# Output product of the state rows: from one full product per row half to seven half-size products

## The chip, the cores and the metric

The kernel runs on one core of a Trainium2 chip. A core has TensorE (PE: matrix products, with a separate weight load PEld that overlaps the products), VectorE (DVE), ScalarE (ACT), GpSimd (POOL) and SyncE (SP, which issues DMAs here); each engine works through its own instructions in program order and waits on semaphores for the others. The metric is the time of one execution on the device in microseconds; less is better.

## The reference

Two stages: a cross attention between 512 token rows and 32 state rows, for 8 batches and 8 heads of 64, and then a gated feed-forward layer over all 4352 rows (8 x 544) of width 512, with an inner width of 1536.

```python
a = softmax(x @ state.T / 8)          # 512 x 32 for each batch and head
xread = a @ state                     # 512 x 64
a2 = softmax(state @ x.T / 8)         # 32 x 512
sread = a2 @ x                        # 32 x 64: the state rows
rows = concatenate([xread, sread])    # 544 rows a batch, 512 wide over the heads
gate = 1 / (1 + exp(-(rows @ w_gate)))
out = (gate * (rows @ w_val)) @ w_out # 4352 x 512, float32
```

## The kernel before, in words

The program is written in a fixed order: what stands first in the code is issued first on its engine, and nothing reorders it. Batches 0 to 7 of token rows are followed by a ninth "batch" `b == B` (B is 8), which holds the state rows of all eight batches together: 8 x 32 = 256 rows. `step(b, f)` handles one of the 12 blocks of 128 of the inner width for one batch. For `b == B` it issues the two products of gate and value (`gv_half`, four matmuls of 256 columns each, line 388), the tanh on ScalarE (`gv_th`, line 394) and the gated product on VectorE (`gv_glu`, line 406, two instructions of 128 columns); the result is `glus[B]`, with 12 blocks of 256 rows.

Between these, every step carries a piece of the output product of the batch before it, so that for `b == B` it is the output product of batch 7. For batches 1 to 7 this is not done as one product: the rows (two halves of 256), the inner width (even and odd blocks f) and the output columns (two halves of 256) are each cut in two, and the eight products of quarters are replaced by seven (`prod`, `w_mm`; Winograd's form). That needs sums of quarters of the weights (`T`, made once by `t_sum`), sums of quarters of the glu blocks (`Sm`, four of them, `s_sum`, line 448), and additions of products as they leave PSUM (`w_keep` on ScalarE, `w_add` on VectorE, line 474). The last product of batch 7's second half is cut in three parts (`p_mm`, line 485, `p_add`, line 491).

The state rows, 256 of them, get no such treatment. After the last step, `out_mm(B, k)` runs for k from 0 to 5: for each half c of 128 rows, 12 matmuls of 512 columns accumulate one PSUM tile (line 422), ScalarE halves it into SBUF (line 426), and SP stores the 256 KB (line 432). Batch 0, which `out_mm` also serves, has another order of k. Behind that come the last three parts of batch 7 (`p_mm(4, part)`), whose additions on VectorE and stores from ACT, SP and ACT are the end of the program. Ahead of `out_mm(B, ...)` stand one addition of batch 7 (`w_add(5, "U2", ...)`, line 474) and the two stores that it allows (line 505).

PSUM places have names: `GV` (two buffers, used by gate and value in turn), `SWP` (four), `OU` and `AT` (one each). In a step for `b == B` the value product of step f takes the `GV` buffer that the gated product of step f-1 has read, so TensorE waits for VectorE there.

Of the kernel before, what the change touches and what calls it, by code (L numbers as in the profile page):

```python
# [8 lines left out]
FP = mybir.dt.float32  # L9
BF = mybir.dt.bfloat16  # L10
AF = mybir.ActivationFunctionType
ALU = mybir.AluOpType
# [4 lines left out]
def kernel(  # L17
# [29 lines left out]
    fp = ctx.enter_context(tc.tile_pool(name="fp", bufs=3))  # L47
# [293 lines left out]
    def sw_wide(b, v, other=AT):  # L341

        if b not in SWs:
            SWs[b] = fp.tile((128, 2, 2, dff), BF, name="SW", bufs=2)
        lo = 768 * v
        for k, places in enumerate(((OU, other), (SWP, SWP), (SWP, SWP))):
            pss = [p[0].tile((128, 512), FP, name="swp", tag=p[1]) for p in places]
            if k < 2:
                sw_mm(pss, b, k, lo, 512, 0)
            else:  # L350
                sw_pair(pss, b, lo + 512, 256)
            for e in range(2):
                if k < 2:
                    sw_left[b, v, k, e] = (SWs[b][:, e, k, lo:lo + 512], pss[e])
                else:
                    sw_left[b, v, k, e] = (SWs[b][:, e, :, lo + 512:lo + 768], pss[e].rearrange("p (w n) -> p w n", w=2))

    def sw_cp(b, lo, w, e, cp):
        cp(*sw_left.pop((b, lo, w, e)))  # L359
# [50 lines left out]
    def rows_of(b, c):  # L410
        return out[b * SC:b * SC + S].rearrange("(p c) n -> c p n", c=4)[c]

    def out_mm(b, k, place=None):
        c, f0 = k // 3, (k % 3) * 4
        if b == 0:

            c, f0 = k // 6 * 2 + k % 2, k % 6 // 2 * 4
        if f0 == 0:
            place = place or (SWP if b == B else OU)
            ops[b, c] = place[0].tile((128, 512), FP, name="outp", tag=place[1])  # L420
        for f in range(f0, f0 + 4):
            nc.tensor.matmul(ops[b, c], glus[b][:, f, c * 128:(c + 1) * 128], wo[:, f],  # L422
                             start=(f == 0), stop=(f == NF - 1))
        if f0 == 8:
            res = fp.tile((128, 512), FP, name="res", bufs=3, padded_shape=(128, 1024))
            nc.scalar.activation(res, ops[b, c], AF.Copy, scale=0.5)
            if b < B:
                n = 512
                for lo in range(0, 512, n):
                    nc.sync.dma_start(rows_of(b, c)[:, lo:lo + n], res[:, lo:lo + n])  # L430
            else:
                nc.sync.dma_start(out.rearrange("(b s) n -> s b n", s=SC)[S:, 4 * c:4 * c + 4], res)

    def A(b, h, r):

        return glus[b].rearrange("p (i r) t -> p r i t", r=2)[:, r, :, h * 256:h * 256 + 256]
# [6 lines left out]
    def s_sum(b, t, half=None):  # L443

        i = slice(0, 6) if half is None else slice(3 * half, 3 * half + 3)
        a, c, op = ((A(b, 1, 0)[:, i], A(b, 1, 1)[:, i], ALU.add), (Sm[:, 0, i], A(b, 0, 0)[:, i], ALU.subtract),
                    (A(b, 0, 0)[:, i], A(b, 1, 0)[:, i], ALU.subtract), (A(b, 0, 1)[:, i], Sm[:, 1, i], ALU.subtract))[t]
        nc.vector.tensor_tensor(Sm[:, t, i], a, c, op)  # L448
# [39 lines left out]
    def p_add(name, part, j):  # L488

        c, lo, n = parts[part]  # L490
        nc.vector.scalar_tensor_tensor(w_res(B - 1, 1)[:, c, j * 256 + lo:j * 256 + lo + n], wps["p", part], 0.5,
                                       held["w", name][:, c, lo:lo + n], ALU.mult, ALU.add)

    wres = {}

    def w_res(b, h):
        if (b, h) not in wres:
            wres[b, h] = fp.tile((128, 2, 512), FP, name="res", bufs=3)
        return wres[b, h]
# [7 lines left out]
    lo_, hi_ = slice(0, 256), slice(256, 512)  # L507
# [373 lines left out]
    def step(b, f):  # L881

        nb, o = (b + 1 if b + 1 < B else None), b - 1
        v, early = f // 6, b == 2
        if nb and f in (0, 6):
            if v:
                rd_mm(nb, AT)
            if early and not v:
                sw_wide(nb, v)
            else:  # L890
                sw_six(nb, v)
            sw_cp(nb, v, 0, 1, act)
# [36 lines left out]
        if f == 7:  # L929
            held["w", "U4"] = fp.tile((128, 2, 256), FP, name="U4", bufs=1)  # L930
            w_add(5, "U2", held["w", "U4"])
        if f == 8 and b < B:
            w_add(7, "U4", w_res(o, 1)[:, :, hi_])
        if f == 9 and b == B:
            for part in range(3):
                p_add("U4", part, 1)
        if f == 10 and b < B:
            w_add(5, "U2", w_res(o, 0)[:, :, hi_])
            w_store(o, 0, nc.sync)
        if f == 11 and b < B:  # L940
            w_add(7, "U2", w_res(o, 1)[:, :, lo_])
            w_store(o, 1, nc.sync)
        if nb:
            if f in (3, 5):
                n_sum(nb, f // 5)
            if f == 6:
                rd_fin(nb)

        if early:
            sums = {0: ((1, None), (2, 1)), 1: ((3, 0),), 2: ((3, 1),)}  # L950
        elif nb:
            sums = {0: ((0, 1), (1, 1)), 1: ((2, 0), (3, 0)), 2: ((2, 1), (3, 1))}
        else:
            sums = {0: ((0, 1),), 1: ((1, 1),), 2: ((2, 0),), 3: ((2, 1),), 5: ((3, 0),), 6: ((3, 1),)}
        for t, i in sums.get(f, ()):
            s_sum(o, t, i)
        if b < B and f in ((9, 11) if b < 6 else (7, 9)):
            s_sum(b, (f - 7) // 2 - (b < 6), 0)

        if nb:  # L960
            if f == 3 + early:
                at_Eb(nb)
            if f == 3 + early or f == 5:
                n_mul(nb, f // 5, pool)
            if f == 3 * early and nb + 2 < B:
                load_x(nb + 2, nc.sync)
            if f == 6:
                aT_dma(nb, 0)
                aT_dma(nb, 1)
                rd_dma(nb)  # L970
                if nb + 1 < B:
                    cast_x(nb + 1, pool, 0, 4)
                    cast_x(nb + 1, pool, 4, 4)
                    at_xT_dma(nb + 1)
                    cast_xs(nb + 1, 0, 4)
                    cast_xs(nb + 1, 4, 4)
            if f == 8 and early:
                for q in range(3):
                    rd_dma(q)
# [7 lines left out]
    w_add(5, "U2", w_res(o, 0)[:, :, hi_])  # L987
    w_store(o, 0, nc.sync)
    w_store(o, 1, nc.sync, cols=hi_)
    for k in range(6):  # L990
        out_mm(B, k, (SWP, OU)[k // 3])
    for part, eng in enumerate((nc.scalar, nc.sync, nc.scalar)):
        c, lo, n = parts[part]
        p_mm(4, part)
# [32 lines left out]
```

## Time and profile before

| what | value |
|---|---|
| median of 3 runs | 214.67 us (214.22 to 215.29) |
| the profiled execution's own time | 214.09 us |
| its span in the trace | 212.3 us |
| granted TensorE clock | 1.0 throughout |
| TensorE busy | 206.2 us, 97% |
| VectorE busy | 158.2 us, 75% |
| ScalarE busy | 129.0 us, 61% |

The span is what the trace covers; 1.8 us of the execution lie around it. Rows of the trace give a start in microseconds from the span's start, a duration, the engine, the line of the kernel, the output and its inputs, how many instructions are merged, and in brackets how long the engine stood idle before it and what ended that. Matmuls are pipelined: one of 256 columns is shown with 273 ns, but the next one starts much earlier.

### The profile page before, as it was taken

How to read it: one execution, taken by the hardware profiler on the slowest of the kernel's cores; microseconds unless marked ns; L12 is line 12 of the kernel's file. 1: busy time of each engine (PE TensorE's matmuls, PEld its weight loads, DVE VectorE, ACT ScalarE, POOL GpSimd, SP SyncE). 2: the span in 40 equal slices, each digit the busy share in tenths (PEclk: the TensorE clock that was granted, in tenths of full speed). 3: DMA queues.
4: the chain of work that ended last, by engine and by line, in shares of the span. 5: the costliest groups of instructions: out<-in, count | busy, mean ns of one | idle time of the engine just before them, and what ended most of it. 6: DMA issues, size and time to landing. Idle time of an engine off the chain costs nothing.

```text
span 212.3 us, 5235 instructions
## 1 busy us (share of the span) xinstructions
PE 206.2 (97%) x2053; PEld 126.3 (59%) x2057; DVE 158.2 (75%) x300; ACT 129.0 (61%) x243; POOL 72.8 (34%) x101
## 2 busy tenths in 40 slices
PE   8998999999999999999999999999999999999992
PEld 3553433544665656666656565656566666788842
DVE  6796897686975779777976798688968778777621
ACT  4897696586877467855786578647864543333211
POOL 7999170259155304650446033802410000000000
PEclk9999999999999999999999999999999999999999
DMA  6999999685498235945911640247010400220043
GB/s 176 206 197 201 275 224 169 93 299 91 92 271 224 60 70 181 242 64 138 313 51 37 98 198 15 43 88 212 14 40 30 177 2 0 99 102 0 3 175 121
DMA packets 40152, 27.01 MB, mean 127 GB/s; under 512 B 23616, under 2 KB 37184, under 8 KB 40128
## 3 DMA queue, kind: packets, MB, share of 16 engines
q1 hardware_dynamic: 29376, 18.69, 33.4%
q0 software_dynamic: 10320, 7.67, 21.8%
q10 hardware_dynamic: 432, 0.33, 0.6%
q8 instruction: 16, 0.26, 0.5%
q14 instruction: 8, 0.07, 0.1%
HBM read 18.35 MB, written 8.91 MB: 128 GB/s over the span
## 4 chain that ended last, share of the span: by engine, by line
PE 89%; DMA 5%; POOL 3%; issue 1%; ACT 1%; DVE 0%; POOLq 0%; ACTq 0%
PE gvp L385 35%; PE outp L466 29%; PE outp L422 7%; PE gvp L388 5%; DMA wgv<-in_moe_w_gate_dram 5%; PE swp L306 4%; PE gvp L373 3%; PE swp L322 2%; POOL wgv L107 2%; PE Sp L154 1%; PE outp L485 1%; POOL xf L103 1%; PE rdp L282 1%; PE rdp L285 0%; ACT SW L359 0%
## 5 line engine op out<-in xcount | busy, mean ns | idle before, releaser
L394 ACT ACTIVATE th<-gvp 128x512 f32<-128x512 f32 (+1 forms) x108 | 62.1, 577 | 52.5 <-PE gvp L385 36.2
L385 PE MATMUL gvp<-aT,SW 128*128 128x512 bf16 x352 | 93.2, 379 | 0.1
L400 DVE SCALAR_TENSOR_TENSOR glu<-th,gvp 128x512 bf16<-128x512 f32 x96 | 65.2, 685 | 30.4 <-PE gvp L385 14.7
L359 ACT CAST SW<-swp 128x512 bf16<-128x512 f32 (+1 forms) x83 | 45.4, 581 | 8.8 <-PE swp L306 7.6
L385 PEld LDWEIGHTS <-SW 128*128 128x128 bf16 x352 | 32.2, 98 | 25.1 <-issue 6.3
L466 PEld LDWEIGHTS <-Sm 128*128 128x128 bf16 x324 | 31.7, 98 | 12.6
L206 POOL CAST Eb<-E 128x256 bf16<-128x256 f32 x32 | 17.5, 580 | 47.5 <-ACT E L174 47.5
L466 PE MATMUL outp<-tw,Sm 128*128 128x256 bf16 x240 | 31.8, 273 | 0.0
L466 PEld LDWEIGHTS <-glu 128*128 128x128 bf16 x240 | 23.5, 98 | 10.2
L466 PE MATMUL outp<-wo,glu 128*128 128x256 bf16 x168 | 22.9, 273 | 0.0
L233 POOL TENSOR_TENSOR ab<-E,ri 128x512 bf16<-128x512 f32 x14 | 14.7, 1051 | 19.8 <-DVE ri L216 19.8
L422 PE MATMUL outp<-wo,glu 128*128 128x512 bf16 x68 | 16.5, 379 | 0.2
L448 DVE TENSOR_TENSOR Sm<-glu 128x768 bf16<-128x768 bf16 (+1 forms) x27 | 15.5, 576 | 0.0
L474 DVE SCALAR_TENSOR_TENSOR res<-outp,U 128x512 f32<-128x512 f32 x19 | 13.0, 685 | 0.0
L388 PE MATMUL gvp<-XS,wgv 128*128 128x256 bf16 x96 | 12.6, 273 | 0.0
L406 DVE SCALAR_TENSOR_TENSOR glu<-th,gvp 128x128 bf16<-128x128 f32 x24 | 8.7, 462 | 5.1 <-PE gvp L388 5.1
L174 ACT ACTIVATE E<-Sp 128x512 f32<-128x512 f32 x15 | 9.1, 604 | 4.9 <-PE Sp L154 3.8
L422 PEld LDWEIGHTS <-glu 128*128 128x128 bf16 x72 | 6.8, 98 | 8.4 <-issue 0.8
L123 POOL CAST xb<-xf 128x1024 bf16<-128x1024 f32 x11 | 11.1, 1037 | 1.4 <-DMA xf<-in_x_dram 1.3
L359 DVE CAST SW<-swp 128x512 bf16<-128x512 f32 (+1 forms) x17 | 10.1, 623 | 2.0 <-PE swp L322 1.7
L466 PE MATMUL outp<-wo,Sm 128*128 128x256 bf16 x84 | 11.5, 273 | 0.0
L214 DVE TENSOR_REDUCE rs<-E 128x16 f32<-128x512 f32 x15 | 10.2, 677 | 1.1 <-ACT E L174 1.1
(93 smaller groups left out, 195.4 us busy)
## 6 DMA issues: line engine op xcount, KB each, us to landing
out_dram<-res SPq DMA_DIRECT2D x13, 512.0 KB, 2.9
xf<-in_x_dram SPq DMA_DIRECT2D x4, 1024.0 KB, 8.5
xf<-in_x_dram POOLq DMA_DIRECT2D x2, 1024.0 KB, 8.9
out_dram<-res SPq DMA_DIRECT2D x7, 256.0 KB, 3.0
wo<-in_moe_w_out_dram POOLq DMA_DIRECT2D x3, 512.0 KB, 11.7
wgv<-in_moe_w_gate_dram POOLq DMA_DIRECT2D x4, 256.0 KB, 7.7
wgv<-in_moe_w_val_dram POOLq DMA_DIRECT2D x4, 256.0 KB, 7.7
xf<-in_x_dram SPq DMA_DIRECT2D x3, 256.0 KB, 3.6
```

The source lines that it names most:

```text
L123: cp(xbs[b].rearrange("p c h d -> p h c d")[:, lo:lo + n], (xhs if b in xhs else xfs)[b][:, lo:lo + n])
L206: nc.gpsimd.tensor_copy(Ebs[b][:, c], E1s[b][:, c])
L233: (nc.gpsimd if eng is pool else nc.vector).tensor_tensor(half(b, i, abs_), e1, ri.unsqueeze(len(ri.shape)).to_broadcast(e1.shape), ALU.mult)
L359: cp(*sw_left.pop((b, lo, w, e)))
L385: nc.tensor.matmul(ps, SWs[b][:, g, w, fs], aTs[b][:, :, g], start=(g == 0), stop=(g == 1))
L388: nc.tensor.matmul(ps, (wg, wv)[w][:, j, fs], XS[:, :, j], start=(j == 0), stop=(j == 3))
L394: nc.scalar.activation(th, held["gv", b, f][0], AF.Tanh, scale=0.5)
L400: nc.vector.scalar_tensor_tensor(glus[b][:, f], held["th", b, f], 1.0, held["gv", b, f][1], ALU.add, ALU.mult)
L422: nc.tensor.matmul(ops[b, c], glus[b][:, f, c * 128:(c + 1) * 128], wo[:, f], start=(f == 0), stop=(f == NF - 1))
L448: nc.vector.tensor_tensor(Sm[:, t, i], a, c, op)
L466: nc.tensor.matmul(wps[key][:, c], lhs[:, i, c * 128:(c + 1) * 128], rhs[:, i], start=(first and c == 0 and i == 0), stop=(i == NF // 2 - ...
L474: nc.vector.scalar_tensor_tensor(to, wps[key], 0.5, held["w", name], ALU.mult, ALU.add)
```

## The change

The output product of the 256 state rows is done by the same seven products. Rows are cut into two halves of 128, the inner width into even and odd blocks, the columns into two halves of 256. `b_mm(k)` issues product k as 6 matmuls of 256 columns. `b_sum(t, lo, hi)` makes blocks lo to hi of the t-th of the four sums of glu blocks (128 columns a block); pieces of them stand at the ends of steps 7 to 11 of `b == B`. The sums lie in a tile named `SW`, of which the state rows had none before. `b_keep` copies and halves a PSUM tile on ScalarE (256 columns), `b_add` adds one to it on VectorE, and `b_store` stores the two halves of rows, both from SP. `out_mm` now serves batch 0 alone.

```diff
-    def out_mm(b, k, place=None):
-        c, f0 = k // 3, (k % 3) * 4
-        if b == 0:
-
-            c, f0 = k // 6 * 2 + k % 2, k % 6 // 2 * 4
+    def out_mm(b, k, place=OU):
+        c, f0 = k // 6 * 2 + k % 2, k % 6 // 2 * 4
...
-            else:
-                nc.sync.dma_start(out.rearrange("(b s) n -> s b n", s=SC)[S:, 4 * c:4 * c + 4], res)
+            nc.sync.dma_start(rows_of(b, c), res)
...
+    def AB(h, r):
+        return glus[B].rearrange("p (i r) t -> p r i t", r=2)[:, r, :, h * 128:h * 128 + 128]
+
+    def b_sum(t, lo, hi):
...
+        SmB = SWs[B][:, :, :, :128]
+        a, c, op = ((AB(1, 0), AB(1, 1), ALU.add), (SmB[:, 0], AB(0, 0), ALU.subtract),
+                    (AB(0, 0), AB(1, 0), ALU.subtract), (AB(0, 1), SmB[:, 1], ALU.subtract))[t]
+        nc.vector.tensor_tensor(SmB[:, t, lo:hi], a[:, lo:hi], c[:, lo:hi], op)
+
+    def b_mm(k, place=None):
+        SmB = SWs[B][:, :, :, :128]
+        lhs, rhs = {1: (AB(0, 0), W[:, 0, 0]), 2: (AB(0, 1), W[:, 1, 0]), 3: (SmB[:, 3], W[:, 1, 1]), 4: (AB(1, 1), T[:, 3]),
+                    5: (SmB[:, 0], T[:, 0]), 6: (SmB[:, 1], T[:, 1]), 7: (SmB[:, 2], T[:, 2])}[k]
...
+        ps = bps[k] = bps[{6: 1, 3: 5, 4: 7}.get(k, k)]
+        for i in range(NF // 2):
+            nc.tensor.matmul(ps, lhs[:, i], rhs[:, i], start=(place is not None and i == 0), stop=(i == NF // 2 - 1),
+                             skip_group_check=True)
+
+    def b_keep(name, k):
+        bk[name] = fp.tile((128, 512), FP, name="th")[:, :256]
+        nc.scalar.activation(bk[name], bps[k], AF.Copy, scale=0.5)
+
+    def b_add(k, name, to=None):
...
+        nc.vector.scalar_tensor_tensor(to, bps[k], 0.5, bk[name], ALU.mult, ALU.add)
+
+    def b_store(c, eng):
+        eng.dma_start(out.rearrange("(b s) n -> s b n", s=SC)[S:, 4 * c:4 * c + 4], w_res(B, 0)[:, c])
...
+        if b == B and f in (7, 8, 9, 10):
+            b_sum(f - 7, 0, 3)
+        if b == B and f == 10:
+            b_sum(0, 3, 5)
+            b_sum(1, 3, 5)
+        if b == B and f == 11:
+            b_sum(0, 5, 6)
+            b_sum(1, 5, 6)
+            b_sum(2, 3, 6)
+            b_sum(3, 3, 6)
...
-    for k in range(6):
-        out_mm(B, k, (SWP, OU)[k // 3])
+    r = w_res(B, 0)
+    b_mm(1, AT)
+    b_keep("V1", 1)
+    b_mm(2, SWP)
+    b_add(2, "V1", r[:, 0, lo_])
+    b_mm(6)
+    b_keep("U2", 1)
+    b_mm(5, GV)
+    b_add(5, "U2")
+    b_mm(7, GV)
+    b_add(7, "U4", r[:, 1, hi_])
+    b_mm(3)
+    b_add(5, "U2", r[:, 0, hi_])
+    b_store(0, nc.sync)
+    b_mm(4)
+    b_add(7, "U2", r[:, 1, lo_])
+    b_store(1, nc.sync)
```

TensorE, from the end of the last step to the last parts of batch 7, before. Each pair is a weight load and its matmul; `outp_3499` and `outp_3515` are the two row halves, `outp_3410` is the first part of batch 7.

```order
L388 LDWEIGHTS wgv_89 [waits DVE_49]
L388 MATMUL gvp_3489<-XS_93,wgv_89 128x256 [waits PE_49]
...
L422 LDWEIGHTS glu_3244
L422 MATMUL outp_3499<-wo_90,glu_3244 128x512
...
L422 LDWEIGHTS glu_3244 [waits DVE_49]
...
L422 MATMUL outp_3515<-wo_90,glu_3244 128x512 [waits PE_49]
...
L485 MATMUL outp_3410<-tw_91,glu_3021 128x256
```

The same place now, where `outp_3511`, `outp_3520`, `outp_3536` and `outp_3545` are the PSUM tiles of products 1 and 6, 2, 5 and 3, 7 and 4, in the order 1, 2, 6, 5, 7, 3, 4, and `SW_3403` holds the sums.

```order
L507 MATMUL outp_3511<-wo_90,glu_3244 128x256
...
L507 LDWEIGHTS glu_3244 [waits DVE_49]
L507 MATMUL outp_3520<-wo_90,glu_3244 128x256
...
L507 MATMUL outp_3511<-tw_91,SW_3403 128x256 [waits Activation_49]
...
L507 LDWEIGHTS SW_3403 [waits DVE_49]
...
L507 MATMUL outp_3536<-tw_91,SW_3403 128x256
...
L507 MATMUL outp_3545<-tw_91,SW_3403 128x256 [waits PE_49]
...
L507 MATMUL outp_3536<-wo_90,SW_3403 128x256 [waits DVE_49]
...
L507 MATMUL outp_3545<-tw_91,glu_3244 128x256 [waits DVE_49]
...
L476 MATMUL outp_3412<-tw_91,glu_3021 128x256
```

In place of 24 matmuls of 512 columns stand 42 of 256, and where one wait for VectorE stood, there are one for ScalarE (product 6, on V1's copy), two for the sums, and two for additions that must have read a PSUM tile before products 3 and 4 add to it.

VectorE at steps 9 and 10, before (line 491 adds the parts of product 7 of batch 7, line 406 is the gated product of step 10, then of step 11):

```order
L491 TENSOR_SCALAR res<-outp,U_3401 128x256 [waits DMAHW6_49,DVE_49]
L491 TENSOR_SCALAR res<-outp,U_3401 128x128 x2
L406 TENSOR_SCALAR glu<-th,gvp 128x4x32 [waits PE_49,Activation_49]
L406 TENSOR_SCALAR glu<-th,gvp 128x4x32
L406 TENSOR_SCALAR glu<-th,gvp 128x4x32 [waits PE_49,Activation_49]
```

And now, where lines 482 and 495 are `p_add` and `b_sum`:

```order
L482 TENSOR_SCALAR res<-outp,U_3401 128x128 x2
L495 TENSOR_TENSOR SW<-glu 128x3x128
L406 TENSOR_SCALAR glu<-th,gvp 128x4x32 [waits PE_49,Activation_49]
L406 TENSOR_SCALAR glu<-th,gvp 128x4x32
L495 TENSOR_TENSOR SW<-glu,SW 128x3x128 [waits DVE_49]
L495 TENSOR_TENSOR SW<-glu 128x2x128 [waits DVE_49]
L495 TENSOR_TENSOR SW<-SW,glu 128x2x128 [waits DVE_49]
L406 TENSOR_SCALAR glu<-th,gvp 128x4x32 [waits PE_49,Activation_49]
```

One sum of three blocks has come between batch 7's additions and step 10's gated product, and three sums between the gated products of steps 10 and 11.

VectorE from the last step to the end, before (line 406 is the gated product of step 11, line 474 the addition of batch 7 that two stores wait for):

```order
L406 TENSOR_SCALAR glu<-th,gvp 128x4x32 [waits PE_49,Activation_49]
L406 TENSOR_SCALAR glu<-th,gvp 128x4x32
L474 TENSOR_SCALAR res<-outp,U_3356 128x2x256
L491 TENSOR_SCALAR res<-outp,U_3356 128x256 [waits PE_49]
L491 TENSOR_SCALAR res<-outp,U_3356 128x128 [waits PE_49] x2
```

And now (line 495 is `b_sum`, 517 `b_add`, 465 and 482 are what 474 and 491 were):

```order
L406 TENSOR_SCALAR glu<-th,gvp 128x4x32
L495 TENSOR_TENSOR SW<-glu 128x128 [waits DVE_49]
L495 TENSOR_TENSOR SW<-SW,glu 128x128 [waits DVE_49]
L495 TENSOR_TENSOR SW<-glu 128x3x128
L495 TENSOR_TENSOR SW<-glu,SW 128x3x128 [waits DVE_49]
L465 TENSOR_SCALAR res<-outp,U_3356 128x2x256
L517 TENSOR_SCALAR res<-outp,th 128x256 [waits DMAHW7_49,PE_49,Activation_49]
L517 TENSOR_SCALAR th<-outp,th 128x256 [waits PE_49,Activation_49]
L517 TENSOR_SCALAR res<-outp,th 128x256 [waits DVE_49,PE_49]
L517 TENSOR_SCALAR res<-outp,th 128x256 [waits PE_49] x2
L482 TENSOR_SCALAR res<-outp,U_3356 128x256 [waits PE_49]
L482 TENSOR_SCALAR res<-outp,U_3356 128x128 [waits PE_49] x2
```

Four sums now stand between the last gated product and batch 7's addition, and five additions of 256 columns ahead of the last three. ScalarE has two copies of 256 columns where it had two of 512. SP's last five stores are the same and in the same order.

More of the change, by code (lines that the diff above doesn't have):

```diff
@@ L411, in rows_of @@
         return out[b * SC:b * SC + S].rearrange("(p c) n -> c p n", c=4)[c]
-    def out_mm(b, k, place=None):
-        c, f0 = k // 3, (k % 3) * 4
-        if b == 0:
-            c, f0 = k // 6 * 2 + k % 2, k % 6 // 2 * 4
+    def out_mm(b, k, place=OU):
+        c, f0 = k // 6 * 2 + k % 2, k % 6 // 2 * 4
         if f0 == 0:
-            place = place or (SWP if b == B else OU)
             ops[b, c] = place[0].tile((128, 512), FP, name="outp", tag=place[1])
@@ L426, in out_mm @@
             nc.scalar.activation(res, ops[b, c], AF.Copy, scale=0.5)
[L427 to L430, printed above, removed]
-            else:
-                nc.sync.dma_start(out.rearrange("(b s) n -> s b n", s=SC)[S:, 4 * c:4 * c + 4], res)
+            nc.sync.dma_start(rows_of(b, c), res)
     def A(b, h, r):
@@ L492, in p_add @@
                                        held["w", name][:, c, lo:lo + n], ALU.mult, ALU.add)
+    def AB(h, r):
+        return glus[B].rearrange("p (i r) t -> p r i t", r=2)[:, r, :, h * 128:h * 128 + 128]
+    def b_sum(t, lo, hi):
+        if B not in SWs:
+            SWs[B] = fp.tile((128, 4, NF // 2, 256), BF, name="SW", bufs=2)
+        SmB = SWs[B][:, :, :, :128]
+        a, c, op = ((AB(1, 0), AB(1, 1), ALU.add), (SmB[:, 0], AB(0, 0), ALU.subtract),
+                    (AB(0, 0), AB(1, 0), ALU.subtract), (AB(0, 1), SmB[:, 1], ALU.subtract))[t]
+        nc.vector.tensor_tensor(SmB[:, t, lo:hi], a[:, lo:hi], c[:, lo:hi], op)
+    bps, bk = {}, {}
+    def b_mm(k, place=None):
+        SmB = SWs[B][:, :, :, :128]
+        lhs, rhs = {1: (AB(0, 0), W[:, 0, 0]), 2: (AB(0, 1), W[:, 1, 0]), 3: (SmB[:, 3], W[:, 1, 1]), 4: (AB(1, 1), T[:, 3]),
+                    5: (SmB[:, 0], T[:, 0]), 6: (SmB[:, 1], T[:, 1]), 7: (SmB[:, 2], T[:, 2])}[k]
+        if place:
+            bps[k] = place[0].tile((128, 512), FP, name="outp", tag=place[1])[:, :256]
+        ps = bps[k] = bps[{6: 1, 3: 5, 4: 7}.get(k, k)]
[6 more added lines that the diff above has]
+    def b_add(k, name, to=None):
+        if to is None:
+            to = bk["U4"] = fp.tile((128, 512), FP, name="th")[:, :256]
+        nc.vector.scalar_tensor_tensor(to, bps[k], 0.5, bk[name], ALU.mult, ALU.add)
+    def b_store(c, eng):
+        eng.dma_start(out.rearrange("(b s) n -> s b n", s=SC)[S:, 4 * c:4 * c + 4], w_res(B, 0)[:, c])
     wres = {}
```

## The prediction

> **What bounds the kernel now.** I read the page first: the busy shares and the chain that ended last.
>
> ```profile
> PE 206.2 (97%) x2053; PEld 126.3 (59%) x2057; DVE 158.2 (75%) x300; ACT 129.0 (61%) x243; POOL 72.8 (34%) x101
> PE 89%; DMA 5%; POOL 3%; issue 1%; ACT 1%; DVE 0%; POOLq 0%; ACTq 0%
> ```
>
> TensorE is busy for 97% of the span and holds 89% of the chain, so a matmul saved counts unless a wait takes its place. The change lies in the last five steps and behind them; I asked for the chain there.
>
> ```profile
> 202.11 5.13 PE outp L422 x23
> 207.24 1.34 PE outp L485 x18
> ...
> 208.60 0.29 DVE res L491
> ```
>
> Without a gap the chain runs through the 24 matmuls that the change replaces (one record is missing), the last parts of batch 7 and their last addition. Behind that only a store is left. The timeline has the other engines.
>
> ```profile
> 196.56 0.71 DVE L474 SCALAR_TENSOR_TENSOR U<-outp,U 128x512 f32<-128x512 f32 x1
> 197.56 0.73 DVE L406 SCALAR_TENSOR_TENSOR glu<-th,gvp 128x128 bf16<-128x128 f32 x2 [0.28 <-PE gvp L388]
> 199.11 0.73 DVE L406 SCALAR_TENSOR_TENSOR glu<-th,gvp 128x128 bf16<-128x128 f32 x2 [0.81 <-PE gvp L388]
> 199.64 0.84 DVE L491 SCALAR_TENSOR_TENSOR res<-outp,U 128x256 f32<-128x256 f32 x3
> 199.93 1.04 PE L388 MATMUL gvp<-XS,wgv 128*128 128x256 bf16 x8
> 200.63 0.73 DVE L406 SCALAR_TENSOR_TENSOR glu<-th,gvp 128x128 bf16<-128x128 f32 x2 [0.16 <-PE gvp L388]
> 201.41 0.36 PEld L388 LDWEIGHTS <-wgv 128*128 128x128 bf16 x4
> 201.46 0.60 PE L388 MATMUL gvp<-XS,wgv 128*128 128x256 bf16 x4
> 202.16 0.73 DVE L406 SCALAR_TENSOR_TENSOR glu<-th,gvp 128x128 bf16<-128x128 f32 x2 [0.80 <-PE gvp L388]
> 202.69 0.71 DVE L474 SCALAR_TENSOR_TENSOR res<-outp,U 128x512 f32<-128x512 f32 x1
> 203.43 0.81 SPq L505 DMA_DIRECT2D out_dram<-res  x2
> 204.68 0.60 ACT L426 ACTIVATE res<-outp 128x512 f32<-128x512 f32 x1 [3.25 <-PE outp L422]
> 205.31 3.14 SPq L432 DMA_DIRECT2D out_dram<-res  x2
> 207.07 1.49 PE L485 MATMUL outp<-tw,glu 128*128 128x256 bf16 x18
> 207.93 0.96 DVE L491 SCALAR_TENSOR_TENSOR res<-outp,U 128x256 f32<-128x256 f32 x3 [4.52 <-PE outp L485]
> 208.38 0.87 ACTq L505 DMA_DIRECT2D out_dram<-res  x2
> ```
>
> VectorE has nothing from 203.40 to 207.93, ScalarE hardly more: that is the cover for the added work behind the last step. In the steps the cover is thin: step 10's gated product begins 0.16 us after VectorE came free and ends at 201.36, and the weight load that waits for it starts at 201.41. The trace does not show whether even those 0.05 us are to spare.
>
> **The matmuls.** The row with eight shows that matmuls of 256 columns start (1.04 - 0.273) / 7 = 0.1096 us apart; 0.273 is the length of one, from the groups by shape.
>
> ```profile
> L466 PEld LDWEIGHTS <-Sm 128*128 128x128 bf16 x324 | 31.7, 98 | 12.6
> L388 PE MATMUL gvp<-XS,wgv 128*128 128x256 bf16 x84 | 11.0, 273 | 0.0
> L422 PE MATMUL outp<-wo,glu 128*128 128x512 bf16 x23 | 5.1, 379 | 0.1
> L394 ACT ACTIVATE th<-gvp 128x256 f32<-128x256 f32 x11 | 4.2, 384 | 11.0 <-PE gvp L388 11.0
> L491 DVE SCALAR_TENSOR_TENSOR res<-outp,U 128x256 f32<-128x256 f32 x2 | 0.9, 437 | 4.5 <-PE outp L485 4.5
> ```
>
> Those of 512 start (5.13 - 0.379) / 22 = 0.2160 us apart. Removed: 24 x 0.2160 = 5.18 us. Added: 42 x 0.1096 = 4.60 us. Without waits that is -0.58 us, all on the path. Weights change before every matmul in both groups, so the added loads are in the 0.1096.
>
> The Trainium skill, "TensorE: Matmul & The Clock Gate", section "Back-to-back issue gap", says that a stream of pairs of weight load and matmul settles at about 81 ns a pair for 128 columns and 131 ns for 512. Estimated in a straight line between them, 256 columns cost 98 ns, and the change would go from 24 x 0.131 = 3.14 to 42 x 0.098 = 4.12 us: 1.0 us more in place of 0.58 less. The trace disagrees: 216 ns for 512 columns in such a stream.
>
> **The sums.** The trace has no sum of 384, 256 or 128 elements; it has the same operation at 768 and 1536, and rows that show how one instruction follows another.
>
> ```profile
> L448 DVE TENSOR_TENSOR Sm<-Sm,glu 128x768 bf16<-128x768 bf16 x12 | 6.7, 555 | 0.1
> L448 DVE TENSOR_TENSOR Sm<-Sm,glu 128x1536 bf16<-128x1536 bf16 x1 | 1.0, 953 | 0.0
> 144.69 0.55 DVE L448 TENSOR_TENSOR Sm<-glu 128x768 bf16<-128x768 bf16 x1
> 145.27 0.56 DVE L448 TENSOR_TENSOR Sm<-Sm,glu 128x768 bf16<-128x768 bf16 x1
> 157.50 0.68 DVE L474 SCALAR_TENSOR_TENSOR U<-outp,U 128x512 f32<-128x512 f32 x1
> 158.10 0.55 DVE L448 TENSOR_TENSOR Sm<-glu 128x768 bf16<-128x768 bf16 x1
> ```
>
> (953 - 555) / 768 = 0.518 ns an element, so 157 ns are fixed: estimates of 356, 290 and 223 ns for 384, 256 and 128 elements. The bound above is a length that does not shrink, 555 ns. The bound below is no fixed part at all: 199, 133 and 66 ns. I take the line, since two sizes lie on it. An instruction that reads what the one before wrote starts 0.03 us after its end (145.27 behind 144.69 + 0.55); one that does not starts some 0.08 us before it (158.10 against 158.18).
>
> **In the steps.** Step 7: the addition to U4 ends at 197.27, the sum runs from 197.19 to 197.55, the gated product of step 8 comes at 197.56: no delay. Behind step 8 VectorE was free for 0.81 us. Step 9: the three additions end at 200.48, the sum runs from 200.40 to 200.76, and step 10's gated product starts near 200.69 instead of 200.63; with 0.05 us or nothing to spare, TensorE then waits up to 0.06 us. I take 0.05. Step 10: three sums, 0.356 + 0.290 + 0.03 + 0.290, fit between 201.21 and 202.16 within a few hundredths, and of step 11's gated product nothing waits before product 2's last weight load.
>
> **Behind the steps**, by 0.1096 us from 201.46 + 4 x 0.1096 = 201.90: product 1 at 201.90, 2 at 202.56, 6 at 203.22, 5 at 203.87, 7 at 204.53, 3 at 205.19, 4 at 205.85, batch 7's parts at 206.50. What each waits for:
> - Product 6 adds to the tile that ScalarE copies as V1. Product 1 ends at 202.45 + 0.27 = 202.72, the copy at 0.03 to 0.08 later takes 0.384 us and ends at 203.13 to 203.18: against 203.22 a wait of 0 to 0.05, I take 0.03.
> - The sums of step 11 on VectorE, with the 0.05 from above: gated product to 202.94, then 202.97 to 203.19, 203.22 to 203.44, 203.36 to 203.72 and 203.64 to 204.00. Product 6's last weight is wanted at 203.77, product 7's fourth at 204.86: both covered, with 0.3 us or more.
> - Product 3 adds to product 5's tile after VectorE has read it. Ahead of that reading stand batch 7's addition (203.94 to 204.65) and b_add of product 2 (204.57 to 205.01); the reading runs from 204.93 to 205.37 at 0.437 us each, and TensorE goes on at 205.40. Product 3 would be ready at 205.19 + 0.05 + 0.03 = 205.27: a wait of 0.13 us. This is the place where the gain leaks.
> - Product 4 waits for the reading of 7: product 7 ends at 205.43, the reading at 205.91, and product 4 would start at 206.06: no wait.
>
> Batch 7's parts then start at 206.50 + 0.05 + 0.03 + 0.13 = 206.71 instead of 207.07. The remaining additions on VectorE (products 3 and 4) end near 207.35, before part 0 needs it at 207.57, as 207.93 does now. Sum: -0.58 + 0.05 + 0.03 + 0.13 = **-0.37 us**.
>
> **The stores.** Batch 7's 512 KB and 256 KB wait for the addition that moves from 202.69 to 203.94: issued at 204.7 instead of 203.43. The state rows' first half moves from 205.31 to 206.8, their second from 207.90 to 207.4; the three parts move 0.36 us forward with TensorE.
>
> ```profile
> 204.00:205.00 1.00, 1.00 (x6) 0.47 (x5) 0.00 (x0) 0.32 (x1) 0.00 (x0) 1.00 0.80 307
> 205.00:206.00 1.00, 1.00 (x7) 0.41 (x6) 0.00 (x0) 0.28 (x1) 0.00 (x0) 1.00 0.91 349
> 206.00:207.00 1.00, 1.00 (x6) 0.48 (x5) 0.00 (x0) 0.00 (x0) 0.00 (x0) 1.00 0.75 271
> 207.00:208.00 1.00, 1.00 (x13) 0.86 (x11) 0.07 (x1) 0.60 (x1) 0.00 (x0) 1.00 0.32 121
> 208.00:209.00 1.00, 0.56 (x11) 0.39 (x7) 0.85 (x3) 0.00 (x0) 0.00 (x0) 1.00 0.00 0
> 209.00:210.00 1.00, 0.00 (x0) 0.00 (x0) 0.00 (x0) 0.00 (x0) 0.00 (x0) 1.00 0.88 318
> 210.00:211.00 1.00, 0.00 (x0) 0.00 (x0) 0.00 (x0) 0.00 (x0) 0.00 (x0) 1.00 0.67 207
> out_dram<-res ACTq DMA_DIRECT2D x1, 64.0 KB, 2.4
> ```
>
> The last column is GB/s. Now the bytes come in two bursts with an empty microsecond at 208, and end near 210 + 207/318 = 210.65. After the change they are one stream: 1048 KB (the first four rows) and 525 KB, from about 205.4. At the 349 of a full row it ends at 205.4 + 1573/349 = 209.9, before the last store could land anyway (issued near 208.6 and 2.4 us to landing: 211.0). I take nothing.
>
> The profiled execution would go from 214.09 to 213.72. The median of the runs is 0.58 above it; from 214.67 the same sum gives **214.3 us**. The runs before lie 1.07 us apart, 0.5% of the median, which is about what a measurement can tell from no change; the gain is 0.17%.
>
> **The rivals.**
> - The waits do not appear: V1 in time, step 9's sum covered, VectorE early enough for product 3. Then all of 0.58: 214.1. For it speaks that every wait above is a difference of a tenth or less; against it that VectorE's row of seven instructions has no gap to give. In the Trainium skill, "VectorE: DVE Perf Modes", the table of its errata section gives 58 + elements/2 cycles at 0.96 GHz, an estimate of 260 ns for 384 elements; by it the four last sums are some 0.35 us shorter and the sum is -0.5. The trace does not bear it out at 768 elements, 460 ns by that form against 555.
> - VectorE is later: nothing starts before the end of its predecessor. Four of the starts above overlap by 0.08, so product 5 is read 0.3 us later, 0.13 becomes 0.45, the gain 0.05: 214.6. Against it the row at 158.10.
> - The sums do not shrink, 0.555 us each. Step 9: 0.26 us. Product 6's last weight is late by 0.7, product 3 by 0.9 more: 0.26 + 0.7 + 0.9 + 0.1 - 0.58 = +1.4: 216.0. Against it the two sizes on one line.
> - Slower by the weights: 18 more weight loads that matmuls of 256 columns do not hide. If a load's 98 ns lay bare, 18 x 0.098 = 1.76 - 0.58 = +1.2: 215.9. It decides at a spacing of 5.18 / 42 = 0.123 us. Against it the 0.1096 of the same pairs. The rule on pairs above comes out near here, with 215.9 (+1.0 and the waits); its chance is in this one's.
> - The stores become the end: one stream at the mean of the last burst's two rows, 262 GB/s, ends at 205.4 + 1573/262 = 211.4, 0.75 us later than now: up to 215.4. Against it, a queue with work in hand moved 349.
>
> **How the numbers follow.** The forecast, with waits of 0.1 to 0.4 us: 0.52. No waits: 0.2. Later VectorE: 0.12. Stores: 0.08. Sums that don't shrink: 0.05. Weights: 0.03. The forecast's own range is 214.1 to 214.6. The range for all is 213.6 to 215.2: the runs' own spread of half a microsecond about 214.1 to 214.7, and most of the stores' case; it leaves out the two slow ones and a tenth of the rest. Slower by over 0.5% (above 215.74) are only those two, 0.08. Faster by over 0.5% (below 213.60) is no case, since even the whole 0.58 is half of that; the spread of the runs leaves 0.04. Within 0.5%: 0.88.
>
> **What would show it.** Right: 42 matmuls about 0.11 us apart, batch 7's parts starting near 206.7, the longest wait of TensorE behind the steps at product 3 and on VectorE, one burst of stores. Wrong: a spacing of 0.12 or more, a wait at the weight loads of products 6 or 7, steps 8 to 11 longer than 1.53 us, bytes still moving past 210.7, or the copies on ScalarE ending after 203.3.

## The result, and the profile after

The changed kernel takes 213.70 us (median of 21 runs, 213.49 to 214.68) against 214.55 us of the kernel before beside it (21 runs): ratio 0.9968, 95% interval 0.9957 to 0.9979, that is -0.69 us (-0.92 to -0.45). The ratio is that of the means, 213.86 and 214.54 us; the medians lie 0.85 us apart. It is faster by less than the 0.5% below which the forecast calls two kernels the same. The forecast was 214.3 us, -0.37 us: 213.70 lies in the range for all (213.6 to 215.2), close to its lower end, and below the forecast's own range (214.1 to 214.6). Two later comparisons of the same kernel gave 0.9969 (0.9958 to 0.9981) and 0.9988 (0.9967 to 1.0009); the last alone would not show a difference. Over all runs of both, 39 of the changed kernel and 118 of the kernel before, the medians are 213.76 and 214.30 us and the shortest tenths end at 213.58 and 214.12 us: -0.54 us in both.

The page after looks like the one before; TensorE is busy for 97% of the span and holds 86% of the chain:

```profile
PE 206.5 (97%) x2075; PEld 128.5 (60%) x2075; DVE 162.0 (76%) x315; ACT 128.4 (60%) x243; POOL 73.0 (34%) x101
```

The chain of waits of the changed kernel, its last pieces (start, length, what):

```profile
202.67 4.70 PE outp L507 x42
207.37 1.34 PE outp L476 x18
208.71 0.02 issue
208.73 0.29 DVE res L482
```

Where 5.13 us of line 422 stood (with one of its 24 matmuls missing from the record), 4.70 us of line 507 stand. But step 11's value product comes 0.6 us later than in the execution before, and the profiled execution's time is 214.22 us, no less than the 214.09 us of before. These 0.6 us are lost long before the change begins. The timeline near 54 us, for the changed kernel (ScalarE's cast of half of batch 3's x, the gated product that follows, and TensorE):

```profile
51.40 1.05 ACT L123 CAST xb<-xf 128x1024 bf16<-128x1024 f32 x1 [1.86 <-DMA xf<-in_x_dram]
52.97 1.29 DVE L400 SCALAR_TENSOR_TENSOR glu<-th,gvp 128x512 bf16<-128x512 f32 x2 [2.71 <-ACT th L394]
53.80 0.92 PE L322 MATMUL swp<-wgv,sTc 64*32 64x512 bf16 x8
54.65 1.04 PE L385 MATMUL gvp<-aT,SW 128*128 128x512 bf16 x4
```

And for the kernel before, where that cast did not have to wait:

```profile
49.34 1.04 ACT L123 CAST xb<-xf 128x1024 bf16<-128x1024 f32 x1
50.91 1.29 DVE L400 SCALAR_TENSOR_TENSOR glu<-th,gvp 128x512 bf16<-128x512 f32 x2 [0.74 <-ACT th L394]
53.70 0.40 PE L322 MATMUL swp<-wgv,sTc 64*32 64x512 bf16 x8
54.03 1.04 PE L385 MATMUL gvp<-aT,SW 128*128 128x512 bf16 x4
```

In this execution a load landed late, ScalarE stood 1.86 us before the cast, the tanh behind it was late, VectorE's gated product with it, and TensorE took 0.92 us for eight matmuls that take 0.40: the offset between the two traces goes from 0.10 to 0.62 us there and stays until the state rows' products. The other 0.10 us stand at 26 us already (a row of 14 gate and value products of line 385 starts at 26.54 us, before at 26.44). So one execution against one execution shows the change only from 201.9 us on. There, in the changed kernel's timeline:

```profile
200.25 0.83 DVE L482 SCALAR_TENSOR_TENSOR res<-outp,U 128x256 f32<-128x256 f32 x3
201.01 0.34 DVE L495 TENSOR_TENSOR SW<-glu 128x384 bf16<-128x384 bf16 x1
201.27 0.72 DVE L406 SCALAR_TENSOR_TENSOR glu<-th,gvp 128x128 bf16<-128x128 f32 x2
202.04 0.34 PEld L388 LDWEIGHTS <-wgv 128*128 128x128 bf16 x4
202.50 1.47 PE L507 MATMUL outp<-wo,glu 128*128 128x256 bf16 x12
203.41 0.38 ACT L512 ACTIVATE th<-outp 128x256 f32<-128x256 f32 x1 [1.36 <-PE outp L507]
203.84 2.12 PE L507 MATMUL outp<-tw,SW 128*128 128x256 bf16 x18
205.08 0.41 DVE L517 SCALAR_TENSOR_TENSOR res<-outp,th 128x256 f32<-128x256 f32 x1
205.42 0.42 DVE L517 SCALAR_TENSOR_TENSOR th<-outp,th 128x256 f32<-128x256 f32 x1
205.90 0.81 PE L507 MATMUL outp<-wo,SW 128*128 128x256 bf16 x6
206.55 0.82 PE L507 MATMUL outp<-tw,glu 128*128 128x256 bf16 x6
207.21 1.49 PE L476 MATMUL outp<-tw,glu 128*128 128x256 bf16 x18
```

From 202.50 to 207.21 are 4.71 us; before, from 201.46 + 4 x 0.1096 = 201.90 to 207.07, they were 5.17. Products 1 and 2 take 12 x 0.1096 = 1.315 us, so product 6, at 203.84, waited 0.025 us; the copy V1 ends at 203.79. The 18 matmuls of products 6, 5 and 7 take 1.973 us, so product 3, at 205.90 instead of 205.81, waited 0.09 us. Product 4 did not wait. The steps kept their length: VectorE's gated product of step 10 now follows the sum directly, 0.73 us behind the matmuls at 200.54 instead of 0.70, and the weight load that waits for it starts 0.02 us later (1.50 us behind them instead of 1.48), but its matmul does not: it starts at 202.07, 1.53 us behind the one at 200.54, as before.

### The profile page after: what moved, and what is told of

Read it like the earlier page. It is cut to its first block, busy times and chain, and to the rows that moved or that the text cites. A ratio compares the mean times of both kernels' runs of the same rounds, so it can differ in the third digit from the quotient of the medians.

```text
span 212.4 us, 5290 instructions
## 1 busy us (share of the span) xinstructions
PE 206.5 (97%) x2075; PEld 128.5 (60%) x2075; DVE 162.0 (76%) x315; ACT 128.4 (60%) x243; POOL 73.0 (34%) x101
## 4 chain that ended last, share of the span: by engine, by line
PE 86%; DMA 8%; ACT 2%; issue 1%; DVE 1%; SPq 0%; ACTq 0%
PE gvp L385 36%; PE outp L457 29%; DMA xf<-in_x_dram 8%; PE gvp L388 5%; PE swp L306 4%; PE outp L507 2%; PE outp L418 2%; PE swp L322 2%; PE gvp L373 1%; PE outp L476 1%; PE Sp L154 1%; PE rdp L282 1%; DVE glu L400 1%; ACT th L394 1%; PE Sp L163 0%
## 5 line engine op out<-in xcount | busy, mean ns | idle before, releaser
L457 PEld LDWEIGHTS <-glu 128*128 128x128 bf16 x240 | 23.5, 98 | 10.2
L418 PE MATMUL outp<-wo,glu 128*128 128x512 bf16 x48 | 11.5, 379 | 0.0
L271 POOL CAST xs<-xf 128x1024 bf16<-128x1024 f32 x10 | 10.2, 1043 | 0.0
```

What stands on the lines that cost most here:

```text
L457: nc.tensor.matmul(wps[key][:, c], lhs[:, i, c * 128:(c + 1) * 128], rhs[:, i], start=(first and c == 0 and i == 0), stop=(i == NF // 2 - ...
```

## The experiments

Two questions were open: whether the 0.46 us behind the steps are all, the rest of the -0.69 us being how executions differ ahead of the change (theory A; theory B gives all of it to the change); and what holds product 3. "Span" is what a trace covers; each run has one, so kernels can also be compared by their shortest spans: 212.3 us for the kernel before, but for one of 97 runs at 212.1, and 211.7 us for the changed one.

**The kernel before against itself, and the changed kernel again.** No edit.

> The kernel before once more, against itself: what a comparison shows when nothing is changed. Theory A (the change is worth what the trace shows behind the steps, 5.17 us to 4.71 us = -0.46 us, and the rest of the measured -0.69 us is how often a run loses half a microsecond near 54 us, where a load of batch 3's x can land late): ratio 1.000, interval no narrower than 0.1%, and single runs in two groups about 0.5 us apart. Theory B (all of the -0.69 us is the change's): ratio 1.000 with an interval that stays well inside 0.1%, one group of runs.

> The changed kernel once more. Theory A: ratio near 1 - 0.46/214.5 = 0.9979, so 0.997 to 0.9985; if its profiled execution has batch 3's load in time (ScalarE's cast at 49 us without a wait), its span is near 211.9 us, and from the start of the state rows' products to batch 7's last parts it is 4.71 us again. Theory B: 0.9968 again, with the 0.2 us more to be found somewhere between the steps and the end.

Measured: the kernel before against itself 0.9992 (0.9982 to 1.0001), medians 214.20 and 214.35 us, spans from 212.3 us in both. A comparison with nothing changed can thus be 0.15 us off, and its interval is wider than theory B had it. Two groups half a microsecond apart show only faintly: 9 of the 11 runs lie at 214.09 to 214.31 us, two at 214.61 and 214.64. The changed kernel again: 0.9969 (0.9958 to 0.9981) with only 6 runs, spans from 211.9 us. Against the two medians of the kernel before beside it, 214.20 and 214.35 us, the changed kernel's 213.76 us is -0.44 or -0.59 us. Its timeline, with batch 3's load in time:

```profile
202.24 1.47 PE L507 MATMUL outp<-wo,glu 128*128 128x256 bf16 x12
203.57 2.12 PE L507 MATMUL outp<-tw,SW 128*128 128x256 bf16 x18
205.63 0.81 PE L507 MATMUL outp<-wo,SW 128*128 128x256 bf16 x6
206.94 1.49 PE L476 MATMUL outp<-tw,glu 128*128 128x256 bf16 x18
```

4.70 us again, with the same 0.09 us at product 3. Its start at 202.24 is 0.34 us later than before's; an offset of 0.34 us stands at 26 us already, which is why its span is 212.2 us and not the 211.9 expected. Neither theory is beaten by the ratios alone; the traces give the change 0.46 us.

**Sums alone.** The kernel before with `b_sum` and its calls added, and nothing using them:

```diff
         for t, i in sums.get(f, ()):
             s_sum(o, t, i)
+        if b == B and f in (7, 8, 9, 10):
+            b_sum(f - 7, 0, 3)
+        if b == B and f == 10:
+            b_sum(0, 3, 5)
+            b_sum(1, 3, 5)
+        if b == B and f == 11:
+            b_sum(0, 5, 6)
+            b_sum(1, 5, 6)
+            b_sum(2, 3, 6)
+            b_sum(3, 3, 6)
```

> The kernel before with the sums of the state rows' glu blocks added at the same places, unused: the 24 matmuls of 512 columns stay. It prices the sums and the later stores of batch 7 alone. If the sums are hidden (my prediction costed 0.05 us in the steps, and the trace after shows none): ratio 1.000, steps 8 to 11 of 1.53 us each, and the product of the state rows 5.17 us long. If VectorE holds TensorE up in the steps: 1.0003 to 1.001, with a weight load that waits in step 10. In both, the store of 512 KB is issued about 1.2 us later without moving the end.

Measured: 1.0027 (1.0014 to 1.0041), more than either case. Two things make it up. The time outside the span is 2.10 to 2.21 us in the 12 runs of this kernel, against 1.73 to 1.84 us for the kernel before beside it: about 0.35 us that the trace doesn't see. The shortest span is 212.5 us, 0.2 us longer, and the timeline says where (TensorE and its weight loads behind the steps):

```profile
204.08 0.68 DVE L474 SCALAR_TENSOR_TENSOR res<-outp,U 128x512 f32<-128x512 f32 x1
204.48 0.38 PE L422 MATMUL outp<-wo,glu 128*128 128x512 bf16 x1
204.81 0.10 PEld L422 LDWEIGHTS <-glu 128*128 128x128 bf16 x1 [0.45 <-DVE res L474]
204.82 0.39 PE L422 MATMUL outp<-wo,glu 128*128 128x512 bf16 x1
```

The steps are not longer (matmuls of the steps stay 0.21 or 0.22 us behind those of the kernel before from 192 to 200 us). But the second row half's matmul, due 0.216 us after 204.48, starts at 204.82: its PSUM place is `OU`, which batch 7's addition must have left, and four sums now stand ahead of that addition. The wait is 0.13 us; the product takes 5.31 us (202.11 to 207.42). So the sums do cost, through an instruction behind them, and the changed kernel, whose products lie in `AT`, `SWP` and `GV`, shows no such wait.

**No sums.** The changed kernel with glu blocks in place of the sums, so that it computes another product for the state rows:

```diff
-        lhs, rhs = {1: (AB(0, 0), W[:, 0, 0]), 2: (AB(0, 1), W[:, 1, 0]), 3: (SmB[:, 3], W[:, 1, 1]), 4: (AB(1, 1), T[:, 3]),
-                    5: (SmB[:, 0], T[:, 0]), 6: (SmB[:, 1], T[:, 1]), 7: (SmB[:, 2], T[:, 2])}[k]
+        lhs, rhs = {1: (AB(0, 0), W[:, 0, 0]), 2: (AB(0, 1), W[:, 1, 0]), 3: (AB(0, 1), W[:, 1, 1]), 4: (AB(1, 1), T[:, 3]),
+                    5: (AB(1, 0), T[:, 0]), 6: (AB(1, 1), T[:, 1]), 7: (AB(1, 0), T[:, 2])}[k]
...
-        if b == B and f in (7, 8, 9, 10):
-            b_sum(f - 7, 0, 3)
...
```

> The changed kernel with the sums left out and glu blocks in their place in products 5, 6, 7 and 3, so that the state rows' result is another one; matmuls, copies, additions and stores are the same. If the wait at product 3 (0.09 us in the trace after) comes from VectorE's row of sums, it goes: 42 x 0.1096 = 4.60 us plus 0.03 us for the copy V1, ratio 0.0004 to 0.0005 below that of the changed kernel beside it. If it is only the time from product 5's end to the end of its reading (product 7 alone is no cover), it stays at 0.05 us or more.

Measured: 0.9987 (0.9978 to 0.9996); here, too, 2.07 to 2.19 us lie outside the span, so the spans are what compares: from 211.8 us, against 211.7 to 211.9 in the three comparisons of the changed kernel. The timeline:

```profile
202.17 1.47 PE L506 MATMUL outp<-wo,glu 128*128 128x256 bf16 x12
203.51 2.12 PE L506 MATMUL outp<-tw,glu 128*128 128x256 bf16 x18
205.07 0.42 DVE L516 SCALAR_TENSOR_TENSOR th<-outp,th 128x256 f32<-128x256 f32 x1 [0.91 <-PE outp L506]
205.55 0.81 PE L506 MATMUL outp<-wo,glu 128*128 128x256 bf16 x6
206.86 1.49 PE L476 MATMUL outp<-tw,glu 128*128 128x256 bf16 x18
```

VectorE has been idle for 0.91 us when it reads product 5's tile, and product 3 still comes at 205.55 instead of 203.51 + 1.973 = 205.48: 0.07 us of the 0.09 are there without a single sum (five profiles with all sums show 0.08 or 0.09). All sums together cost the changed kernel at most 0.02 us here, little more than the rounding of these times. What remains is the round trip: from product 5's last matmul, which starts at 203.51 + 11 x 0.1096 = 204.72, to product 3 are 0.83 us (0.27 for that matmul, 0.08 to the reading, 0.42 for it, 0.06 back), and the 0.66 us of product 7 and one spacing of 0.11 us do not cover them.

**Pairs of half the columns.** The kernel before with its 24 matmuls split into 48:

```diff
-            nc.tensor.matmul(ops[b, c], glus[b][:, f, c * 128:(c + 1) * 128], wo[:, f],
-                             start=(f == 0), stop=(f == NF - 1))
+            for lo in ((0, 256) if b == B else (0,)):
+                n = 256 if b == B else 512
+                nc.tensor.matmul(ops[b, c][:, lo:lo + n], glus[b][:, f, c * 128:(c + 1) * 128], wo[:, f, lo:lo + n],
+                                 start=(f == 0 and lo == 0), stop=(f == NF - 1), skip_group_check=True)
```

> The kernel before, with each of the state rows' 24 matmuls of 512 columns split into two of 256, each with its own weight load: 48 pairs for the same product. Theory A (a pair costs what its columns cost, 0.1096 us): 48 x 0.1096 = 5.26 us in place of 5.18, a span 0.1 us longer than that of the kernel before (212.4 against 212.3 at best). Theory of unhidden weight loads: 24 loads of 98 ns more, up to 2.4 us longer; it would have turned the change's sign at 0.123 us a pair, here 5.9 us for the 48.

Measured: 1.0010 (0.9991 to 1.0029), spans from 212.4 us. In the timeline the 48 start at 202.64 and batch 7's parts at 207.88: 5.24 us, 0.1092 us a pair.

```profile
202.64 5.40 PE L424 MATMUL outp<-wo,glu 128*128 128x256 bf16 x48
207.88 1.49 PE L487 MATMUL outp<-tw,glu 128*128 128x256 bf16 x18
```

24 weight loads more cost 0.06 us. The theory of unhidden loads has fallen. By the rule of the Trainium skill ("TensorE: Matmul & The Clock Gate", "Back-to-back issue gap") a pair of 256 columns would cost about three quarters of one of 512 (98 to 131 ns, the former an estimate between its figures). The trace does not agree: here it costs 0.506 of it, 0.1092 us to 0.216.

**Two sums done twice.** One pair of lines added to the changed kernel:

```diff
             b_sum(2, 3, 6)
             b_sum(3, 3, 6)
+            b_sum(2, 3, 6)
+            b_sum(3, 3, 6)
```

> The changed kernel with the last two sums of step 11 done a second time: some 0.55 us more on VectorE ahead of batch 7's addition. If VectorE's row is what product 3 waits for, the wait there grows from 0.09 us by nearly all of that, to 0.6 us, and the shortest span goes from 211.75 to 212.3 us. If, as the run without sums says, the row has just enough room, the first few hundredths are free and the rest counts: a wait of 0.55 to 0.6 us. If VectorE is not what matters there, nothing changes.

Measured: 1.0028 (1.0009 to 1.0047). The trace shows the wait at product 3 that was expected:

```profile
205.45 0.41 DVE L517 SCALAR_TENSOR_TENSOR th<-outp,th 128x256 f32<-128x256 f32 x1
205.91 0.81 PE L507 MATMUL outp<-wo,SW 128*128 128x256 bf16 x6 [0.44 <-DVE th L517]
207.22 1.49 PE L476 MATMUL outp<-tw,glu 128*128 128x256 bf16 x18
```

From 202.01 to 207.22 are 5.21 us, 0.5 us more: of 0.53 us of added work (0.27 us from one sum's start to the next) all but a few hundredths come through. VectorE's row has no more room than that; the sums are hidden, but just so. The shortest span, 212.8 us, is 1.1 us above the changed kernel's, twice what this explains. In the profiled execution the other half stands at the end: the span ends 3.97 us behind the last addition, where it is 3.3 to 3.5 us in the others, and the last store of 64 KB lands 2.9 us after its issue instead of 2.4. Why, no run here shows.

**Without the stores of batch 7 that its addition releases.** The two `w_store` calls ahead of the state rows' products are left out, so those rows are not written.

```diff
     w_add(5, "U2", w_res(o, 0)[:, :, hi_])
-    w_store(o, 0, nc.sync)
-    w_store(o, 1, nc.sync, cols=hi_)
```

> The changed kernel without the two stores of batch 7 that wait for its addition (768 KB less to write; those rows of the output stay unwritten). If the one stream of stores at the end sets the end, the last landing comes earlier by 0.1 us or more against the last addition on VectorE (3.4 us from the last addition's end to the end of the span, before and after); if the end is the last store's own landing time, that stays 3.3 to 3.4 us and the spans stay at 211.75 us at best.

Measured: 0.9981 (0.9962 to 1.0000), spans from 211.9 us, and the span ends 3.5 us behind the last addition (208.64 to 212.1), as in the changed kernel (208.75 to 212.2 in its second profile). These two stores do not set the end. The bytes in the second profile of the changed kernel, by microsecond (last column GB/s), run together as the prediction said:

```profile
206.00:207.00 1.00, 1.00 (x12) 0.90 (x10) 0.59 (x2) 0.00 (x0) 0.00 (x0) 1.00 1.01 397
207.00:208.00 1.00, 1.00 (x15) 0.93 (x14) 0.63 (x2) 0.00 (x0) 0.00 (x0) 1.00 0.78 275
208.00:209.00 1.00, 0.42 (x8) 0.25 (x5) 0.71 (x3) 0.00 (x0) 0.00 (x0) 1.00 0.76 279
209.00:210.00 1.00, 0.00 (x0) 0.00 (x0) 0.00 (x0) 0.00 (x0) 0.00 (x0) 1.00 1.00 361
210.00:211.00 1.00, 0.00 (x0) 0.00 (x0) 0.00 (x0) 0.00 (x0) 0.00 (x0) 1.00 0.50 148
```

They end near 210 + 148/361 = 210.4, before the last landing.

**Batch 3's cast behind a tanh.** In the opening part of the program, which the change does not touch:

```diff
-    cast_x(3, act, 0, 4)
     gv_mm(1, 0, SWP)
-    at_xT_dma(3)
     gv_th(1, 0)
+    cast_x(3, act, 0, 4)
+    at_xT_dma(3)
```

> The changed kernel with ScalarE's cast of half of batch 3's x issued behind the tanh of batch 1's block 0 instead of ahead of it. Theory A says that executions lose up to 0.5 us near 54 us when that load lands late, because the tanh stands behind the cast. Then the shortest spans stay at 211.7 to 211.8 us, and the longer ones (over 212.1; 6 of the first 21) become rare: median about 0.1 us lower, ratio 0.996 to 0.997. If the spread comes from the start alone (the first 26 us), nothing changes.

Measured: 0.9978 (0.9961 to 0.9995), median 213.75 us, spans from 211.9 us. Theory A's expectation fails: the median was expected 0.1 us below the changed kernel's 213.70 and 213.76 us, and is not; spans above 212.1 us were expected to become rare, and are 3 of 11 where they were 6 of 21. The late load is shown for one execution, the first profile of the changed kernel. The traces say that it does not make most of the spread: in each of the ten other profiles the offset to the first profile of the kernel before is at 202 us what it was at 27 us, within 0.02 us, and it is anything from 0.01 to 1.1 us. So those executions differ in their first 27 us, as this experiment's other theory said; what differs there was not tried.

**A part of batch 7 between products 7 and 3**, and the changed kernel beside it:

```diff
     b_mm(7, GV)
     b_add(7, "U4", r[:, 1, hi_])
+    p_mm(4, 2)
+    p_add("U2", 2, 0)
+    w_store(o, 1, nc.scalar, slice(1, 2), slice(128, 256))
     b_mm(3)
...
-    for part, eng in enumerate((nc.scalar, nc.sync, nc.scalar)):
+    for part, eng in ((0, nc.scalar), (1, nc.sync)):
```

> The changed kernel with one of batch 7's last parts (part 2: 6 matmuls of 128 columns, 0.33 us, with its addition and its store from ACT) put between products 7 and 3; parts 0 and 1 stay last. If the wait at product 3 is the time that the reading of product 5's tile needs behind product 5's end (0.27 us to its end, 0.04 to VectorE, 0.42 to read and 0.06 back, against 0.66 us of product 7), it goes: from the start of the state rows' products to the end of all of batch 7's parts 0.06 to 0.09 us less than in the changed kernel beside it, shortest span 211.7 us, ratio lower by 0.0003 to 0.0004, which the medians can hardly show. If something else holds product 3, the wait stays.

> The changed kernel a third time, beside the run with the part moved. Theory A: spans from 211.75 us at best, median 211.9 to 212.0 us, ratio 0.997 to 0.9985 against the kernel before, whose spans begin at 212.3 us; over all runs of both kernels so far the shortest tenths lie 0.5 us apart, as the traces say (5.17 against 4.71 us). Theory B: 0.7 us apart.

Measured: with the part moved 0.9974 (0.9964 to 0.9984), spans from 211.8 us; the changed kernel 0.9988 (0.9967 to 1.0009), spans from 211.7 us, with 8 of 12 at 212.3 or more. The timeline of the moved part:

```profile
203.00 1.47 PE L507 MATMUL outp<-wo,glu 128*128 128x256 bf16 x12
204.34 2.13 PE L507 MATMUL outp<-tw,SW 128*128 128x256 bf16 x18
206.31 0.50 PE L476 MATMUL outp<-tw,glu 128*128 128x128 bf16 x6
206.64 0.82 PE L507 MATMUL outp<-wo,SW 128*128 128x256 bf16 x6
207.95 1.15 PE L476 MATMUL outp<-tw,glu 128*128 128x256 bf16 x12
```

Part 2 starts at 206.31, where product 7's spacing ends (204.34 + 1.973), and product 3 0.33 us later, with nothing between: the wait is gone. From the first product to the end of the last matmul are 6.10 us, against 6.20 (202.50 to 208.70) in the changed kernel. The gain of 0.1 us is in the trace; the runs do not show it. The medians of 213.72 and 214.24 us lie further apart than any wait here, and the shortest spans the other way round.

The third comparison of the changed kernel misses theory A's expectation: the ratio is 0.9988 (0.997 to 0.9985 were expected) and the median span 212.45 us (211.9 to 212.0). Its profile says where the half microsecond is, by the same row of 14 gate and value products, first of the kernel before, then of this run:

```profile
26.44 3.20 PE L385 MATMUL gvp<-aT,SW 128*128 128x512 bf16 x14
27.00 3.19 PE L385 MATMUL gvp<-aT,SW 128*128 128x512 bf16 x14
```

It is 0.56 us late at 27 us, and 0.55 us late at the state rows' products (202.45 against 201.90). If each offset at 202 us is taken off its span, the three profiles of the changed kernel come to 211.8, 211.9 and 211.85 us, and the two of the kernel before to 212.3: 0.4 to 0.5 us, as theory A has it. The shortest tenths of all runs lie 0.54 us apart, nearer to its 0.5 than to theory B's 0.7. What the other 0.08 us over the traces' 0.46 are, if they are anything, stays open: spans are given to 0.1 us.

## Why the prediction was right, point by point

- *The matmuls, -0.58 us.* Right: 4.71 us less the two waits is 4.60, as 42 x 0.1096; the split kernel had 0.1092 a pair.
- *The sums of 356, 290 and 223 ns.* Right, as the groups by shape of the changed kernel show:

```profile
L495 DVE TENSOR_TENSOR SW<-glu 128x384 bf16<-128x384 bf16 x3 | 1.0, 345 | 0.0
L495 DVE TENSOR_TENSOR SW<-glu 128x256 bf16<-128x256 bf16 x1 | 0.3, 277 | 0.0
L495 DVE TENSOR_TENSOR SW<-glu 128x128 bf16<-128x128 bf16 x1 | 0.2, 226 | 0.0
```

  Sums that also read `SW` take 366 and 384 ns for 384 elements, 293 for 256 and 226 for 128. The line through the two larger sizes held within 8% down to a sixth of the smaller one. The rival of sums that do not shrink is out. The Trainium skill's form of 58 cycles and half a cycle an element ("VectorE: DVE Perf Modes", errata section) gives an estimate of 260 ns for 384 elements; as the length of a sum, the trace does not agree with it (345 to 384 ns). But what a sum adds to VectorE's row is less than its length, since the next one starts before its end: independent sums of 384 start 0.27 us apart (203.94 and 204.21 in the changed kernel), close to that estimate. The prediction had this overlap in its row of starts.
- *In the steps, 0.05 us.* Too much: nothing. Step 10's gated product started 0.03 us later than before (201.27, less the offset of 200.54 - 199.93 = 0.61, is 200.66 against 200.63), not 0.06, and the weight load behind it 0.02 us later without moving its matmul. So the 0.05 us of room were real.
- *The copy V1, 0.03 us.* Right: 0.025.
- *Product 3, 0.13 us.* This is the place, as forecast, but at 0.09 us, and the reason was half wrong. The step read "Ahead of that reading stand batch 7's addition (203.94 to 204.65) and b_add of product 2 (204.57 to 205.01)"; without any sum 0.07 us of the wait stay. The time from product 5's end through its reading is longer than product 7, whoever stands ahead, and the prediction did not work out that time. That VectorE's row has no room beyond that was right: 0.53 us more of sums gave 0.5 us more of waiting.
- *Stores, nothing.* Right, as far as it was tried; 768 KB taken away did not move the end.
- *The sum, -0.37 us.* By the traces -0.575 + 0.025 + 0.09 = -0.46. The mis-sized terms are the step's 0.05 and product 3's 0.13. This lies between the forecast and the rival without waits (-0.58). The first comparison's -0.69 us is more than even that rival allows, so part of it is not the change; the third comparison has -0.26 us, and the kernel before against itself differs by 0.15 us in the median. That the excess comes from how executions differ ahead of the change fits the traces, but is not shown run by run.
- *The time, 214.3 us.* Measured were 213.70, 0.6 us less, and of this the change explains only the 0.09 us above. The forecast started from 214.67 us, the median of three runs; over 118 runs the kernel before has 214.30. This is 0.37 us of the miss. That 213.70 lies inside the range for all is owed to the range's width, and in part to luck.

## What to carry to other kernels

Price a replaced product by start-to-start spacing in its own stream, then look for the accumulation that must wait until a tile has been read: the product between must last longer than end, reading and way back together (here 0.83 us from the last matmul's start, against the 0.77 us that one spacing and product 7 give), and an independent piece of work put there takes the wait away. Added work on an engine off the path is paid by what stands behind it in its queue, here an addition that a PSUM place hung on, though the added instructions themselves delayed nobody. Before a difference of two profiled executions is read, find where their offset begins. And a forecast of a time needs more than three runs of the kernel before, where single runs lie a microsecond apart.

## What was not expected of the hardware

The time outside the span was 1.73 to 1.85 us in every run of the kernel before, the changed one and five others, but 2.07 to 2.21 us in all 24 runs of two builds (sums alone, no sums), though their traces begin alike (TensorE's first matmul at 0.99 us) and end alike (3.3 to 3.4 us behind the last addition). A difference of about 0.35 us between two kernels can thus lie where no trace shows it; what sets it was not tried. The last store of 64 KB took 2.3 to 2.5 us to land in the other profiles and 2.9 us in that of the kernel with two sums done twice, behind nearly the same bytes (385, 345, 233, 370 and 249 GB/s in the microseconds from 206 on, against 389, 348, 227, 369 and 240 in the first profile of the changed kernel).
